# Issuing the first load of w_in ahead of the opening all-engine barrier in a single-token decode kernel

## The chip, the cores and the metric

The kernel runs on one core of a Trainium2 chip. The metric is device time in microseconds (us); lower is better.

## The reference, cut to what matters

One token of width 1024 goes through grouped-query attention over a cache (32 query heads, 4 KV heads, 65,536 positions) and through a gated MLP. A scalar gate mixes the two results.

```python
q = (x @ wq)                                   # wq: 1024 x 4096
scores = einsum(q, k) * Dh ** -0.5             # k_cache: 4 x 65536 x 128, 67 MB
a = (softmax(scores) @ v) @ wo                 # v_cache: 67 MB; wo: 4096 x 1024
z = gelu(x @ w_in)                             # w_in: 1024 x 3584
b = (z[:Fh] * (w_sp * layernorm(z[Fh:]) + b_sp)) @ w_out
out = g * a + (1 - g) * b                      # g = sigmoid(sum(x * gate_w))
```

All is bf16. Nearly every byte of the 162 MB is used once, so this is a kernel that reads memory.

## The kernel before

SyncE issues all big loads into four rotating 4 MB buffers; ScalarE issues four tiny ones. Program order on SyncE is: both halves of w_in, both halves of wq, four K tiles, w_out, then K and V tiles in turn and the last V tiles, and at the end the pieces of wo.

```python
kv = ctx.enter_context(tc.tile_pool(name="kv", bufs=NKV))          # NKV = 4

def load(src, shape, name):
    t = kv.tile([P, CT * P], BF16, name=name, tag="kv")
    ...
    nc.sync.dma_start(out=v, in_=src)
    return v
...
nc.scalar.dma_start(out=xg8[:, 0, :], in_=A_x.rearrange(...))       # 2 KB
nc.scalar.dma_start(out=xg8[:, 1, :], in_=gate_w.rearrange(...))    # 2 KB
nc.scalar.dma_start(out=wb[:, 0:1], in_=B_w_sp)                     # 2 bytes
nc.scalar.dma_start(out=wb[:, 1:2], in_=B_b_sp.unsqueeze(0))        # 2 bytes
win_t = [load(win_view[:, i * KH:(i + 1) * KH, :], (KH, F), "win_t") for i in range(2)]
wq_t = [load(wq_view[:, i * KH:(i + 1) * KH, :], (KH, HD), "wq_t") for i in range(2)]
... # xb_ps: x is spread over the partitions by a matmul; small_ps: w_sp, b_sp and the gate
z_ps = pss.tile([P, 2 * HN], FP32, name="z_ps", tag="s")
for i in range(2):
    x_rows(z_ps, win_t[i], ZN, i)              # 32 matmuls for each half of w_in
... # gelu, layernorm, q_ps from wq_t
build_w(0)
for g in range(G):
    for j in range(NT):
        k_tile(g, j, load_kv(A_k_cache, g, j, "kn"))   # the first one takes win_t[0]'s buffer
        ...
```

The framework puts an opening ahead of this code: GpSimd fills four constants, every engine drains, and an all-engine barrier follows. Only then does each engine reach its first line of the kernel.

## Time and profile before

| | before |
|---|---|
| median time of 3 runs | 385.78 us (385.75 to 385.80) |
| span of the profile | 383.9 us |
| bytes, mean rate | 162.01 MB, 422 GB/s |
| busy: load queue / TensorE / VectorE | 98.5% / 63% / 57% |

The first lines are from the page of the kernel before. The DMA row gives the busy tenths of the 16 DMA engines in 40 slices, and the GB/s row what they moved. Then come SyncE's queue (packets, MB, share of 16 engines' span) and the chain that ended last, by engine and by line.

```profile
span 383.9 us, 2650 instructions
...
DMA  8999999999999999999999999999999999999995
GB/s 335 430 437 437 435 434 430 423 431 426 428 427 437 435 430 437 427 434 430 423 432 427 437 437 422 430 434 437 427 425 427 437 438 427 425 430 431 434 411 203
...
q1 hardware_dynamic: 6192, 162.01, 98.5%
...
DMA 60%; DVE 20%; PE 11%; issue 5%; ACT 2%; SPq 1%; DVEq 0%; ACTq 0%
DMA kn<-in_A_k_cache_dram 47%; DVE kt L320 16%; DMA wo_t<-in_A_wo_dram 8%; PE s_ps L326 8%; DMA win_t<-in_B_w_in_dram 5%; DVE pt L362 2%; PE o_ps L372 2%; ACT sc L337 1%; PE z_ps L213 1%; ACT sc L359 1%; DVE mx L341 1%; DVE o_sb L387 0%; SPq L449 0%; ACT L359 0%; PE nb_ps L352 0%
```

The load queue never pauses after the first slice: the packet records hold no moment without one of its packets. (A slice can read up to 438 GB/s, because a packet counts whole in the slice in which it starts.) The trace's packet records say the same in another way: in the opening loads, once the stream has settled, a 28,672-byte packet occupies one DMA engine for 1.062 us, and 16 of these make 432 GB/s. The Trainium skill ("Perfetto Trace Analysis", Engine Utilization, Roofline) calls about 435 GB/s the ceiling of one core's 16 DMA engines; the trace agrees.

The next lines are from the view of the opening's instructions (engine, operation, count, duration in ns, first and last start in us). The letter q after an engine's name means its sequencer.

```profile
L478 POOLq EVENT_SEMAPHORE  x2: 17/17/17, 0.5 to 0.6; - x2
L478 SPq DRAIN  x1: 7/7/7, 0.0 to 0.0; - x1
...
L478 POOLq DRAIN  x1: 186/186/186, 0.3 to 0.3; - x1
...
L478 SPq EVENT_SEMAPHORE  x1: 17/17/17, 0.7 to 0.7; - x1
```

SyncE is ready at 0.0 us and passes the barrier at 0.7 us. GpSimd fills constants first, drains for 0.19 us from 0.3 us, and does its barrier steps at 0.5 to 0.6 us.

The timeline of the first 32 us of the kernel before (start, busy us, engine, line, operation, and in brackets the idle time before it and what ended it) shows what follows the barrier:

```profile
0.74 0.86 SPq L107 DMA_DIRECT2D win_t<-in_B_w_in_dram  x2
0.74 0.61 ACTq L117 DMA_DIRECT2D xg<-in_A_x_dram  x1
0.82 0.25 POOL L131 IOTA row<- 128x128 f32 x1 [0.38 <-POOLq L478]
...
7.64 0.37 PE L169 MATMUL xb_ps<-xg,spread 8*128 8x256 bf16 x1 [7.64 <-DMA xg<-in_gate_w_dram]
...
11.58 0.16 DVE L185 CAST wbf<-wb 1x2 f32<-1x2 bf16 x1 [2.12 <-DMA wb<-in_B_b_sp_dram]
...
12.30 3.18 PE L213 MATMUL z_ps<-win_t,xT 128*32 128x448 bf16 x32
...
15.54 8.36 SPq L107 DMA_DIRECT2D kn<-in_A_k_cache_dram  x2
20.34 3.18 PE L213 MATMUL z_ps<-win_t,xT 128*32 128x448 bf16 x32 [4.86 <-DMA win_t<-in_B_w_in_dram]
```

And the end of the timeline of the kernel before, where the last piece of wo decides:

```profile
380.69 0.29 PE L414 MATMUL out_ps<-wo_t,oa 128*32 128x256 bf16 x4 [0.36 <-DMA wo_t<-in_A_wo_dram]
381.02 0.37 ACT L453 CAST out_sb<-out_ps 128x256 bf16<-128x256 f32 x1 [47.61 <-PE out_ps L414]
381.43 0.61 ACTq L454 DMA_DIRECT2D out_dram<-out_sb  x1
```

### The profile page before, as it was taken

What the parts mean: (1) busy time and instruction counts of PE and PEld (TensorE: products, weight loads), DVE (VectorE), ACT (ScalarE), POOL (GpSimd) and SP (SyncE); (2) the same over time, 40 slices, a digit from 0 to 9 for tenths busy, and PEclk for the clock granted to TensorE, in tenths of its full rate; (3) what the DMA queues carried; (4) which work ended last, traced back from release to release, by engine and by line L of the source; (5) the groups of instructions that cost most, each with busy time, mean ns of one, the idle gap of its engine ahead of it and who ended that gap; (6) DMA issues with size and microseconds to landing.
All of it is one profiled execution on the core that took longest, in us unless ns stands there. A gap on an engine that the chain in (4) does not pass through costs nothing.

```text
span 383.9 us, 2650 instructions
## 1 busy us (share of the span) xinstructions
PE 242.3 (63%) x1372; PEld 59.3 (15%) x796; DVE 218.5 (57%) x211; ACT 39.6 (10%) x55; POOL 4.4 (1%) x10
## 2 busy tenths in 40 slices
PE   0433447976449948466699393774993937685553
PEld 0110001111202201011121020121220201121122
DVE  5141478988497563658975545679754546730040
ACT  1010001100511101014011010140110101400000
POOL 4000000000000000000000000000000000000000
PEclk9996559889659989686599797865997869888868
DMA  8999999999999999999999999999999999999995
GB/s 335 430 437 437 435 434 430 423 431 426 428 427 437 435 430 437 427 434 430 423 432 427 437 437 422 430 434 437 427 425 427 437 438 427 425 430 431 434 411 203
DMA packets 6248, 162.18 MB, mean 422 GB/s; under 512 B 728, under 2 KB 732, under 8 KB 1116
## 3 DMA queue, kind: packets, MB, share of 16 engines
q1 hardware_dynamic: 6192, 162.01, 98.5%
q8 instruction: 8, 0.13, 0.1%
q14 instruction: 4, 0.03, 0.0%
q10 hardware_dynamic: 44, 0.01, 0.0%
HBM read 162.01 MB, written 0.00 MB: 422 GB/s over the span
## 4 chain that ended last, share of the span: by engine, by line
DMA 60%; DVE 20%; PE 11%; issue 5%; ACT 2%; SPq 1%; DVEq 0%; ACTq 0%
DMA kn<-in_A_k_cache_dram 47%; DVE kt L320 16%; DMA wo_t<-in_A_wo_dram 8%; PE s_ps L326 8%; DMA win_t<-in_B_w_in_dram 5%; DVE pt L362 2%; PE o_ps L372 2%; ACT sc L337 1%; PE z_ps L213 1%; ACT sc L359 1%; DVE mx L341 1%; DVE o_sb L387 0%; SPq L449 0%; ACT L359 0%; PE nb_ps L352 0%
## 5 line engine op out<-in xcount | busy, mean ns | idle before, releaser
L326 PE MATMUL s_ps<-kt,wt 128*128 128x512 bf16 x512 | 142.3, 437 | 67.9 <-DVE kt L320 67.3
L320 DVE STREAM_TRANSPOSE kt<-kn 128x2048 int32<-128x2048 int32 x64 | 143.3, 2284 | 63.5 <-DMA kn<-in_A_k_cache_dram 63.4
L372 PE MATMUL o_ps<-vt,pt 128*64 128x512 bf16 x512 | 69.2, 432 | 8.8 <-DMA vt<-in_A_v_cache_dram 8.8
L326 PEld LDWEIGHTS <-wt 128*128 128x128 bf16 x256 | 27.6, 108 | 184.0 <-issue 122.9
L337 ACT CAST sc<-s_ps 128x1024 bf16<-128x1024 f32 x16 | 16.2, 1013 | 253.8 <-PE s_ps L326 253.8
L372 PEld LDWEIGHTS <-pt 128*64 128x64 bf16 x256 | 17.2, 124 | 57.9 <-issue 56.4
L362 DVE STREAM_TRANSPOSE pt<-sc 128x1024 bf16<-128x1024 bf16 x16 | 18.6, 1218 | 6.8 <-ACT sc L359 6.8
L383 DVE TENSOR_TENSOR om<-o_ps,own 128x1024 f32<-128x1024 f32 x4 | 4.8, 1205 | 26.8 <-PE o_ps L372 26.8
L359 ACT ACTIVATE sc<-sc,nb 128x1024 bf16<-128x1024 bf16 x16 | 18.2, 1139 | 10.2 <-DVE nb L355 10.2
L322 DVE TENSOR_REDUCE mx<-sc 128x1 f32<-128x1024 bf16 x12 | 14.3, 1192 | 4.4 <-ACT sc L337 4.4
L341 DVE TENSOR_REDUCE mx<-sc 128x1 f32<-128x1024 bf16 x4 | 4.9, 1220 | 12.3 <-ACT sc L337 12.3
L213 PE MATMUL q_ps<-wq_t,xT 128*32 128x512 bf16 x64 | 7.2, 630 | 7.3 <-DMA wq_t<-in_A_wq_dram 7.3
L393 PE MATMUL om_ps<-o_sb,hsel 128*32 128x128 f32 x8 | 2.4, 398 | 13.6 <-DVE o_sb L387 13.6
L213 PE MATMUL z_ps<-win_t,xT 128*32 128x448 bf16 x64 | 6.4, 577 | 4.9 <-DMA win_t<-in_B_w_in_dram 4.9
L414 PE MATMUL out_ps<-wo_t,oa 128*32 128x256 bf16 x128 | 6.3, 346 | 4.6 <-DMA wo_t<-in_A_wo_dram 3.2
L279 DVE TENSOR_TENSOR rowt<-q_ps,own_b 128x512 f32<-128x512 f32 x2 | 1.3, 686 | 12.4 <-PE q_ps L213 12.4
L345 PE MATMUL mt_ps<-ident_f,m 128*1 128x128 f32 x4 | 1.4, 346 | 10.2 <-DVE m L343 10.2
L387 DVE TENSOR_REDUCE o_sb<-om 128x128 f32<-128x1024 f32 x4 | 7.5, 1871 | 0.1
L227 DVE TENSOR_TENSOR rowt<-z_ps,own_b 128x448 f32<-128x448 f32 x2 | 1.2, 620 | 9.6 <-PE z_ps L213 9.6
L213 PEld LDWEIGHTS <-xT 128*32 128x32 bf16 x64 | 3.0, 140 | 20.3 <-issue 20.3
L453 ACT CAST out_sb<-out_ps 128x256 bf16<-128x256 f32 x1 | 0.4, 372 | 47.6 <-PE out_ps L414 47.6
L414 PEld LDWEIGHTS <-oa 128*32 128x32 bf16 x128 | 4.2, 119 | 6.9 <-issue 4.2
(88 smaller groups left out, 57.9 us busy)
## 6 DMA issues: line engine op xcount, KB each, us to landing
kn<-in_A_k_cache_dram SPq DMA_DIRECT2D x16, 4096.0 KB, 26.5
vt<-in_A_v_cache_dram SPq DMA_DIRECT2D x16, 4096.0 KB, 32.9
wq_t<-in_A_wq_dram SPq DMA_DIRECT2D x2, 4096.0 KB, 28.4
win_t<-in_B_w_in_dram SPq DMA_DIRECT2D x2, 3584.0 KB, 15.1
wo_t<-in_A_wo_dram SPq DMA_DIRECT2D x1, 4096.0 KB, 27.2
wout_t<-in_B_w_out_dram SPq DMA_DIRECT2D x1, 3584.0 KB
wo_t<-in_A_wo_dram SPq DMA_DIRECT2D x1, 2048.0 KB
wo_t<-in_A_wo_dram SPq DMA_DIRECT2D x1, 1024.0 KB
```

Source lines behind the costliest of these rows:

```text
L213: ins = nc.tensor.matmul(ps[t * B:(t + 1) * B, k * HN:k * HN + n], lhsT=xT[:, i * KH + c:i * KH + c + 1].to_broadcast([P, B]), rhs=w[:, c, ...
L320: nc.vector.transpose(out=kt[:].bitcast(I32), in_=kb[:, v * n:(v + 1) * n])
L322: nc.vector.reduce_max(**late.pop())
L326: ins = nc.tensor.matmul(s_ps[:, k * HN:(k + 1) * HN], lhsT=wt[g % 2][:, v, b].rearrange("p a v h -> p (a v h)"), rhs=kx[:, b // 2, b % 2, ...
L337: nc.scalar.copy(out=sct[g, j][:], in_=s_ps[:])
L341: nc.vector.reduce_max(**late.pop())
L359: nc.scalar.activation(out=sct[g, j][:], in_=sct[g, j][:], func=ACT.Exp, scale=SCALE, bias=nb[:, 0:1], accum_out=lss[g][:, j:j + 1])
L362: nc.vector.transpose(out=ptt[g, j][:].rearrange("p c x -> p (c x)"), in_=sct[g, j][:])
L372: ins = nc.tensor.matmul(o_ps[g][hs, e, :], lhsT=ptt[g, j][:, 2 * u:2 * u + 2, :].rearrange("p c x -> p (c x)"), rhs=vx[:, 2 * u + e], sta ...
L383: nc.vector.tensor_tensor(out=om8[:], in0=o_ps[g][:].rearrange("p e (v d) -> p (e v) d", d=DH), in1=own_8[:].unsqueeze(2).to_broadcast([P, ...
L387: nc.vector.tensor_reduce(out=o_sb[:], in_=om8[:].rearrange("p x d -> p d x"), axis=AX.X, op=ALU.add)
L414: nc.tensor.matmul(out_ps[t * B:(t + 1) * B, :], lhsT=vec[:, c0 + c:c0 + c + 1].to_broadcast([P, B]), rhs=w[:, c, t * NO:(t + 1) * NO], st ...
```

## The change

The intent is to start the stream of loads while the other engines are still on their way to the barrier. The first load writes a fresh buffer and waits for nothing, so its instruction is taken out of the kernel's block and put in front of SyncE's drain in the opening block. That nothing in the opening has to come before this load is shown only by correct results.

```diff
+    first_load = []
+
+    def start_first_load(n):
+        blocks = n.main_func.blocks
+        found = None
+        for block in blocks:
+            for i, ins in enumerate(block.instructions):
+                if ins.name in first_load:
+                    found = (block, i, ins)
+        block, i, ins = found
+        assert not ins.has_wait()
+        del block.instructions[i]
+        head = blocks[0].instructions
+        at = next(i for i, x in enumerate(head)
+                  if x.engine == ins.engine and type(x).__name__ == "InstDrain")
+        head.insert(at, ins)
+
+    nc.at_finalize(start_first_load)
+
     def load(src, shape, name):
...
-        nc.sync.dma_start(out=v, in_=src)
+        ins = nc.sync.dma_start(out=v, in_=src)
+        if not first_load:
+            first_load.append(ins.ins.name)
         return v
```

## The prediction

> **What bounds the kernel now.** The loads. The page's table of DMA queues shows SyncE's load queue occupying the 16 DMA engines for 98.5% of the span, and 162.01 MB move at a mean 422 GB/s. TensorE is busy 63%, VectorE 57%. The chain of waits gives DMA 60% of the span. SyncE waits often (159.1 us for transposes that free K buffers, by its list of waits), but it waits with about three loads queued: a load takes 26 to 33 us from issue to landing, while 4 MB take about 9.8 us at 430 GB/s. The stream is not starved: all stretches of 10 and 20 us between 40 and 370 us show 419 to 444 GB/s.
>
> **What the change does.** Nothing is added or removed. The issue of the first half of w_in (0.38 to 0.43 us of SyncE), moves from behind the opening barrier to the head of SyncE's program. The instruction list shows SyncE's drain at 0.0 us, its barrier wait of 0.7 us, and the issue at 0.74 us. The load waits for nothing, so it can start 0.7 us earlier, at about 0.0 to 0.05 us.
>
> **What lies on the critical path.** All of it: the stream is continuous, so every later transfer, and the compute behind it, should move forward equally. Checks:
> - The second half of w_in will be issued just after the barrier, at about 0.75 us, while the first half needs some 9 us of transfer: no gap.
> - Does SyncE delay the barrier? It now arrives after about 0.45 us. GpSimd, filling constants first, collects the others at 0.5 to 0.6 us: the barrier moves by at most about 0.1 us.
> - What is pushed back: the four tiny loads on ScalarE's queue. The Trainium skill ("DMA: Bandwidth & Descriptors", Queues, rings and completion order) says each DMA engine takes turns between queues at packet granularity. This trace fits: a 28 KB packet takes 1.06 us, gate_w's 2 KB wait until 7.6 us, and b_sp's value until 11.6 us. Now w_in is ahead even of x, so these landings may come 1 to 2 us later, and TensorE's first z matmuls start near 13 instead of 12.3 us. That is harmless: TensorE then sits idle for 4.9 us until the second half lands at 20.3 us, and the first K load, released by the first half's matmuls (15.5 us), has two wq loads queued ahead of it.
> - The tail is bound by the last w_o piece landing (380.64 us), then 0.3 us of matmul, a 0.37 us copy and the output store: it just shifts.
>
> **Prediction.** 385.78 - 0.7 = 385.1 us; range 384.6 to 385.7. Faster by over 2%: 0.01; within 2%: 0.98; slower by over 2%: 0.01.
>
> **What would show the steps right.** First issue near 0.0 us; the second half of w_in lands near 19.6 instead of 20.3 us; the last w_o piece near 379.9 us; the queue's share still about 98.5%. Wrong, if the first packets start late all the same, or if the 0.7 us is seen at 20 us but gone at 380 us.
>
> **What would make it wrong.** A drain on SyncE that waits for its transfer (the barrier would end near 10 us, and the time would rise about 1 to 2 us); an issue before the barrier that is itself slow; the later tiny loads exceeding their 4 us of slack; or a timing that starts with the first instruction and hides part of the shift.

## The result, and the profile after

| | before | after |
|---|---|---|
| median time (4 runs each, same rounds) | 385.79 us | 385.12 us (384.99 to 385.23) |
| ratio, 95% interval | | 0.9982 (0.9968 to 0.9996) |
| span of the profile | 383.9 us | 383.4 us |
| start of the first w_in packet, from the first instruction | 1.74 us | 1.00 us |
| first w_in packet's start to last wo packet's end | 378.43 us | 378.47 us |

A ratio is the mean time of one kernel's runs over that of the other's of the same rounds, so it is not quite the ratio of the medians. The gain is 0.67 us, and the interval excludes 1. The last two rows are worked out from the trace's DMA packet records, counted from the first instruction's record. They carry the whole story: the stream begins 0.74 us earlier and is as long as it was, within 0.04 us.

The page of the kernel after, the same lines:

```profile
span 383.4 us, 2650 instructions
...
DMA  9999999999999999999999999999999999999994
GB/s 374 436 427 427 422 432 431 438 435 437 426 434 424 422 431 434 438 434 431 429 431 427 427 431 433 438 427 427 434 429 424 431 435 434 432 427 428 431 417 193
...
q1 hardware_dynamic: 6192, 162.01, 98.6%
...
DMA 63%; DVE 19%; PE 10%; issue 5%; ACT 1%; SPq 0%; ACTq 0%; DVEq 0%
DMA kn<-in_A_k_cache_dram 53%; DVE kt L341 16%; DMA wo_t<-in_A_wo_dram 8%; PE s_ps L347 6%; DMA wb<-in_B_b_sp_dram 3%; PE o_ps L393 3%; DVE pt L383 1%; ACT sc L358 1%; PE z_ps L234 1%; DVE o_sb L408 0%; SPq L470 0%; ACT sc L380 0%; DVE mx L362 0%; DVE om L404 0%; DVE mx L343 0%
```

The first slice rises from 335 to 374 GB/s, and the rest is as before. In the chain, w_in's 5% is gone and the 2-byte load of b_sp has 3%. It looks as if a tiny load had become a limit; the experiments test that.

The opening's instructions of the kernel after (the same code has line 499 now):

```profile
L499 POOLq EVENT_SEMAPHORE  x2: 17/17/17, 0.6 to 0.7; - x2
...
L499 SPq DRAIN  x1: 126/126/126, 0.4 to 0.4; - x1
L499 SPq EVENT_SEMAPHORE  x1: 17/17/17, 0.7 to 0.7; - x1
```

SyncE now issues first and drains at 0.4 us. The drain takes 126 ns instead of 7 ns, so it does not wait for the transfer.

The timeline of the first 32 us of the kernel after:

```profile
0.00 1.11 SPq L126 DMA_DIRECT2D win_t<-in_B_w_in_dram  x2
...
0.79 0.60 ACTq L138 DMA_DIRECT2D xg<-in_A_x_dram  x1
0.87 0.25 POOL L152 IOTA row<- 128x128 f32 x1 [0.43 <-POOLq L499]
...
9.13 0.36 PE L190 MATMUL xb_ps<-xg,spread 8*128 8x256 bf16 x1 [9.13 <-DMA xg<-in_gate_w_dram]
...
11.98 0.16 DVE L206 CAST wbf<-wb 1x2 f32<-1x2 bf16 x1 [1.04 <-DMA wb<-in_B_b_sp_dram]
...
12.71 3.01 PE L234 MATMUL z_ps<-win_t,xT 128*32 128x448 bf16 x32
...
15.78 7.47 SPq L126 DMA_DIRECT2D kn<-in_A_k_cache_dram  x2
19.68 3.18 PE L234 MATMUL z_ps<-win_t,xT 128*32 128x448 bf16 x32 [3.97 <-DMA win_t<-in_B_w_in_dram]
```

ScalarE's first issue moves from 0.74 to 0.79 us: the barrier is 0.05 us later. The matmul that waits for gate_w is 1.5 us later, the first z matmuls are 0.4 us later, and the second z matmuls, which wait for data of the big stream, are 0.66 us earlier.

The end of the timeline of the kernel after:

```profile
380.02 0.40 PE L435 MATMUL out_ps<-wo_t,oa 128*32 128x256 bf16 x4 [0.25 <-DMA wo_t<-in_A_wo_dram]
380.47 0.37 ACT L474 CAST out_sb<-out_ps 128x256 bf16<-128x256 f32 x1 [47.63 <-PE out_ps L435]
380.88 0.61 ACTq L475 DMA_DIRECT2D out_dram<-out_sb  x1
```

The last four matmuls start 0.67 us earlier. The output store is issued 0.55 us earlier, because these matmuls took 0.40 instead of 0.29 us in the profiled run. The medians of the timed runs differ by 0.67 us.

### The profile page after: what moved, and what is told of

Its sections match the earlier page's. It is cut to its first block, busy times and chain, and to the rows that moved or that the text cites. A ratio compares the mean times of both kernels' runs of the same rounds, so it can differ in the third digit from the quotient of the medians.

```text
span 383.4 us, 2650 instructions
## 1 busy us (share of the span) xinstructions
PE 237.4 (62%) x1372; PEld 58.5 (15%) x796; DVE 218.3 (57%) x211; ACT 39.6 (10%) x55; POOL 4.4 (1%) x10
## 3 DMA queue, kind: packets, MB, share of 16 engines
q1 hardware_dynamic: 6192, 162.01, 98.6%
## 4 chain that ended last, share of the span: by engine, by line
DMA 63%; DVE 19%; PE 10%; issue 5%; ACT 1%; SPq 0%; ACTq 0%; DVEq 0%
DMA kn<-in_A_k_cache_dram 53%; DVE kt L341 16%; DMA wo_t<-in_A_wo_dram 8%; PE s_ps L347 6%; DMA wb<-in_B_b_sp_dram 3%; PE o_ps L393 3%; DVE pt L383 1%; ACT sc L358 1%; PE z_ps L234 1%; DVE o_sb L408 0%; SPq L470 0%; ACT sc L380 0%; DVE mx L362 0%; DVE om L404 0%; DVE mx L343 0%
## 5 line engine op out<-in xcount | busy, mean ns | idle before, releaser
L347 PE MATMUL s_ps<-kt,wt 128*128 128x512 bf16 x512 | 138.1, 425 | 73.5 <-DVE kt L341 73.4
```

The source lines that it names most:

```text
L347: ins = nc.tensor.matmul(s_ps[:, k * HN:(k + 1) * HN], lhsT=wt[g % 2][:, v, b].rearrange("p a v h -> p (a v h)"), rhs=kx[:, b // 2, b % 2, ...
```

## The experiments

The theory is that time follows the start of the big load stream one for one, and that nothing else in the opening counts. The rivals are: the gain is noise; it comes from some early DMA, whichever; the time of the barrier itself matters; later slack absorbs part of a shift; the tiny loads have become a limit, as the chain after suggests. All experiments gave correct results. The hoisting code is that of the change, for a list of instructions instead of one.

### The change again

No edit; five rounds, on the chip of the next three experiments.

> The changed kernel once more, with more rounds, on the chip of the runs below. Theory (the load stream starts 0.74 us earlier and nothing later absorbs it): 0.6 to 0.75 us less than the kernel before, about 385.1 us. Rival (the first measurement's interval nearly touched 1.0, so the gain may be noise): no clear difference.

Measured: 385.14 us (385.08 to 385.18), before 385.84 us (385.67 to 385.91), ratio 0.9982 (0.9968 to 0.9995). It is the same gain on a second set of runs, with no overlap of the two ranges. The noise rival is out.

### Only the tiny load of x is moved

```diff
-    nc.scalar.dma_start(out=xg8[:, 0, :], in_=A_x.rearrange(...))
+    ins = nc.scalar.dma_start(out=xg8[:, 0, :], in_=A_x.rearrange(...))
+    early.append(ins.ins.name)          # hoisted ahead of ScalarE's drain
```

> Only the first tiny load, x on ScalarE's queue, is moved ahead of the barrier; w_in stays behind it. Theory (only the start of the big stream counts): first 28 KB packet no earlier than before, time 385.8 us, or up to 0.15 us more if ScalarE's late arrival delays the barrier. Rival (any early DMA wakes the engines and brings the gain, or the tiny loads are what matters): about 385.1 us.

Measured: 386.38 us (386.10 to 386.47), ratio 1.0013 (1.0001 to 1.0026): 0.54 us more than before. From the timeline and the opening's instructions of this kernel:

```profile
0.14 0.60 ACTq L133 DMA_DIRECT2D xg<-in_A_x_dram  x1
...
1.16 0.88 SPq L123 DMA_DIRECT2D win_t<-in_B_w_in_dram  x2
```

```profile
L495 ACTq DRAIN  x1: 133/133/133, 0.8 to 0.8; - x1
L495 SPq EVENT_SEMAPHORE  x1: 17/17/17, 1.1 to 1.1; - x1
```

ScalarE's issue of x takes 0.60 us, so ScalarE comes last to the barrier, and SyncE's w_in issue, still behind it, moves from 0.74 to 1.16 us. The first w_in packet starts at 2.18 us, 0.44 us later than before. The direction is the theory's; my expectation had the barrier's delay too small (0.15 us), since I had not added ScalarE's start at 0.14, its issue of 0.60 and its drain of 0.13 us. In this profiled run the stream itself was also 0.13 us longer (378.56 us), which was not explained. An early DMA of the wrong kind is a loss.

### All four opening loads of SyncE are moved

The edit is shown against the change.

```diff
-        if not first_load:
-            first_load.append(ins.ins.name)
+        if len(sp_early) < 4:           # w_in twice, wq twice
+            sp_early.append(0)
+            early.append(ins.ins.name)
```

> All four opening loads on SyncE (both halves of w_in, both of wq) are moved ahead of the barrier, so SyncE arrives at it after about 1.8 us. Theory (only the first issue counts, the barrier itself does not): 385.1 us like the change, though the barrier ends near 2 us and the tiny loads come over 1 us later. Rival (a later barrier costs its delay): about 386.2 us, or at least 0.5 us more than the change.

Measured: 385.12 us (384.98 to 385.15), ratio 0.9981 (0.9968 to 0.9993). From the opening's instructions and the timeline of this kernel:

```profile
L497 SPq EVENT_SEMAPHORE  x1: 17/17/17, 2.2 to 2.2; - x1
```

```profile
2.30 0.60 ACTq L136 DMA_DIRECT2D xg<-in_A_x_dram  x1
...
17.15 0.33 SPq L123 DMA_DIRECT2D kn<-in_A_k_cache_dram  x1
```

The barrier ends at 2.2 us in this kernel's opening, ScalarE's first issue is at 2.30 us, and the first K load is issued at 17.15 us instead of 15.78 us. None of this costs anything. So a barrier 1.5 us later than the change's is free as long as the stream is already ahead of it. Together with the previous run this separates the two: the barrier matters only through what it holds back.

### The opposite dose: the first load issued late

```diff
+    rowt = big.tile([P, 2 * HN], FP32, name="rowt")      # moved up from below
+    nc.vector.memset(rowt[:], 0.0)
+    for _ in range(3):
+        nc.scalar.copy(out=rowt[:], in_=rowt[:])
...
         t = kv.tile([P, CT * P], BF16, name=name, tag="kv")
+        if not seen:
+            seen.append(0)
+            nc.scalar.copy(out=t[:, 0:1], in_=rowt[:, 0:1])   # the load must wait for this write
```

> The opposite dose on the kernel before: the first w_in load waits for three 1 us copies on ScalarE, so it is issued near 7 us instead of 0.74 us. Theory (the start of the stream counts one for one): time = 385.8 + (issue - 0.74), about 392.1 us for an issue at 7.0 us. Rival (much of a shift at the start is absorbed by slack later): less than 389 us.

Measured: 392.11 us (392.05 to 392.14), ratio 1.0162. From the timeline of this kernel:

```profile
7.04 0.84 SPq L112 DMA_DIRECT2D win_t<-in_B_w_in_dram  x2
```

The first issue was at 7.04 us and the first packet at 8.03 us. That is 6.29 us later than before, and the time is 6.27 us more. Nothing later absorbs a shift at the start, even one more than eight times as large as the change's.

### The change with all tiny loads moved too

```diff
     # on top of the change: each of the four tiny loads on ScalarE
+    early.append(ins.ins.name)
```

> The change, and the four tiny loads on ScalarE moved ahead of the barrier too. After the change the chain of waits runs through the landing of b_sp's value at 11.9 us and the first z matmuls to the first K load at 15.8 us. Theory (that part of the chain has slack, because two wq loads are still queued): 385.1 us, no gain over the change even if the first z matmuls start earlier. Rival (the chain shows a real limit): the time falls by about as much as the z matmuls start earlier, 0.5 us or more below the change.

Measured: 385.18 us (385.00 to 385.26), ratio 0.9983 (0.9970 to 0.9995). From the timeline of this kernel:

```profile
11.73 3.18 PE L236 MATMUL z_ps<-win_t,xT 128*32 128x448 bf16 x32
...
14.97 0.33 SPq L123 DMA_DIRECT2D kn<-in_A_k_cache_dram  x1
```

The first z matmuls start at 11.73 instead of 12.71 us and the first K load is issued at 14.97 instead of 15.78 us, but the time does not fall. What the chain of waits shows between 2 and 16 us is not a limit.

### The change with the tiny loads issued late

```diff
+    rowt = big.tile([P, 2 * HN], FP32, name="rowt")
+    nc.vector.memset(rowt[:], 0.0)
+    for _ in range(8):                  # 28 in the second kernel
+        nc.scalar.copy(out=rowt[:], in_=rowt[:])
     xg8 = const.tile([KC, 2, P], BF16, name="xg8")
     nc.scalar.dma_start(...)            # the four tiny loads follow
```

> The change, with the four tiny loads issued behind eight 1 us copies on ScalarE, near 11 us instead of 0.8 us; b_sp's value should land near 20 us and the first K load be issued near 24 us instead of 15.8. Theory (the K load only has to be queued before the wq loads run out near 38 us): 385.1 us. Rival 1 (the slack is the 4 us of TensorE's idle time before the second z half, as the prediction said): about 5 us more, 390 us. Rival 2 (the chain of waits shows a real limit): about 8 us more, 393 us.

Measured: 385.13 us (384.98 to 385.23), ratio 0.9982 (0.9968 to 0.9995). The timeline of this kernel:

```profile
21.63 5.89 PE L238 MATMUL z_ps<-win_t,xT 128*32 128x448 bf16 x64
24.86 3.04 SPq L126 DMA_DIRECT2D kn<-in_A_k_cache_dram  x2
```

The z matmuls start 8.9 us and the first K load 9.1 us later than in the change, and the time is the same within 0.02 us. So the "4 us of slack" of the prediction was far too small.

> The same with 28 copies: the tiny loads are issued near 31 us, land near 40 us, and the first K load is issued near 44 us. Theory (the stream runs dry near 38 us and waits): a hole of about 6 us in the DMA after 38 us and about 6 to 7 us more time, 391 to 392 us. Rival (slack of 4 us): about 25 us more, 410 us.

Measured: 394.09 us (393.74 to 395.22), ratio 1.0219 (1.0206 to 1.0233), 8.95 us more than the change by the medians. Here the slack does end. The view by windows of this kernel (window, its length, then busy us and count of PE, PEld, DVE, ACT and POOL, the granted clock, the DMA share and GB/s; a packet counts whole in the window in which it starts, so a share can exceed 1):

```profile
37.00:38.00 1.00, 0.00 (x0) 0.00 (x0) 0.00 (x0) 0.00 (x0) 0.00 (x0) 1.00 0.84 361
38.00:39.00 1.00, 0.00 (x0) 0.00 (x0) 0.00 (x0) 0.00 (x0) 0.00 (x0) 1.00 0.02 1
39.00:45.00 6.00, 4.19 (x37) 1.86 (x25) 2.66 (x16) 0.17 (x1) 0.00 (x0) 1.00 0.00 0
45.00:46.00 1.00, 1.00 (x16) 0.16 (x4) 0.00 (x0) 0.00 (x0) 0.00 (x0) 1.00 0.00 0
46.00:47.00 1.00, 1.00 (x16) 0.16 (x4) 0.00 (x0) 0.00 (x0) 0.00 (x0) 1.00 1.68 459
```

The last wq packet ends at 38.63 us, and the first K packet starts at 46.39 us: a hole of 7.8 us, and a K start 8.33 us later than the change's 38.06 us. I had expected 6 to 7 us. The K load was issued at 45.42 instead of near 44 us, and I had left out the 0.98 us from issue to first packet. For the remaining 0.6 us (8.95 - 8.33), the packet records of the profiled run point to the restart of the stream: counted from the first K packet, in order of their starts, packet 16 is 8.86 us, packet 128 8.92 us and packet 256 8.93 us later than the same packet of the change. This profiled run, the slowest of the four (395.22 us), loses about 1 us more among its last 128 packets (9.01 to 10.08 us later); why it does was not traced.

### The runs together

| kernel | first w_in packet, us | shift against before | median time, us | difference to before of the same rounds |
|---|---|---|---|---|
| before | 1.74 | 0 | 385.84 | 0 |
| after (again) | 1.00 | -0.74 | 385.14 | -0.70 |
| four opening loads early | 1.00 | -0.74 | 385.12 | -0.72 |
| change, tiny loads early too | 0.99 | -0.75 | 385.18 | -0.66 |
| change, tiny loads 8 copies late | 1.01 | -0.74 | 385.13 | -0.71 |
| only x early | 2.18 | +0.44 | 386.38 | +0.54 |
| first load late | 8.03 | +6.29 | 392.11 | +6.27 |

The packet starts are from one profiled run each. Over seven kernels the time follows the start of the stream to within about 0.1 us. The kernel with 28 copies is the one that leaves this line, and it does so because the stream itself has a hole. No version was found that beats the change by more than the scatter: SyncE's first instruction is already the load.

## Why the prediction was right

The predicted time was 385.1 us; 385.12 and 385.14 us were measured.

- **The bound.** The load stream was named as the bound; the shift carried to the end (0.74 us at the first packet, 0.70 at the last, 0.67 in the time), and the late load shows the same for a shift of 6.29 us. Right, and shown.
- **The 0.7 us.** The issue moved from 0.74 to 0.00 us and the first packet from 1.74 to 1.00 us. Right, and shown. The other checks that it named came out too: the z matmuls that wait for the second half of w_in start at 19.68 us, the last piece of wo has landed at 379.98 us, and the queue's share is 98.6%. The Trainium skill ("DMA: Bandwidth & Descriptors", Latency and other measured facts) gives a first-byte time of about 0.6 us for this kind of queue; here the first packet starts 1.00 us after the issue starts, and 0.63 us after it ends (the issue took 0.38 us).
- **The barrier.** At most 0.1 us later was predicted; 0.05 us was measured. The feared drain took 126 ns. That its time does not matter was only implied; the run with four loads shows it.
- **The tiny loads.** 1 to 2 us later was predicted. It was 1.5 us for gate_w, but only 0.4 us for b_sp, so the first z matmuls started at 12.71 and not near 13 us. The packet records show where b_sp caught up. The value of w_sp, the 4-byte packet behind it, b_sp's value and its 4-byte packet start at 7.85, 9.01, 10.08 and 11.14 us before, one to each big packet's time of 1.06 us, but at 9.42, 10.49, 10.50 and 11.56 us after: two of them go together, which saves one such turn. Why they did was not tested.
- **The slack.** This step was mis-sized. The prediction took TensorE's idle time of 4.9 us before the second z half as the limit ("4 us of slack"). The eight-copy run used up 9 us at no cost; the limit is the moment when the queued wq loads run out, 38.6 us. The prediction had named these queued loads in the same sentence and should have used them.
- **The tail.** "It just shifts" held for the landing of wo (0.66 us); in the profiled pair 0.11 us was lost in the last matmuls. The profiled run of the change (385.20 us) is the second slowest of its four; the medians give 0.67 us.

## What to carry to other kernels

Where a continuous stream of loads is the bound, its first issue is on the critical path, and a load that waits for nothing does not have to stand behind an opening barrier: moving it gave nearly all of the 0.74 us that it had waited, 0.67 and 0.70 us in two sets of runs. Choose the engine and the load with care, because an early issue on an engine that then comes late to the barrier delays everything that is still behind it (0.54 us lost with the tiny load of x). And don't take the chain of waits as a list of limits: ask how much is queued at the DMA engines, for here a load issued behind two others was late by 9 us and cost nothing.

## What the Trainium skill lacked or had wrong

- No page tells that a DMA without waits may be issued before a program's opening barrier, or what that is worth: 0.67 to 0.70 us here. The place would be "DMA: Bandwidth & Descriptors", Rules for kernel authors.
- "Perfetto Trace Analysis" names a drain as an instruction of the sequencer but does not say whether a drain behind a DMA issue waits for the transfer. Here it did not: 126 ns on SyncE and 133 ns on ScalarE behind one issue, 125 ns and 239 ns behind four, against 7 to 8 ns without one.
- "DMA: Bandwidth & Descriptors", Queues, rings and completion order, states the turns between queues but no cost. Here two loads of 2 KB and two of 2 bytes ran beside a stream of 28 KB packets (1.06 us each), and the copy that waits for the last of them started 10.8 us after the first was issued (0.74 to 11.58 us) in the kernel before, and 11.3 us after (9.62 to 20.90 us) in the run with eight copies. Without the stream beside them, in the run with the first load late, the last packet of the same four loads ended at 2.88 us instead of 11.15 us.
- The first-byte figure of about 0.6 us on the same page fits the SyncE loads looked at only if it is counted from the end of the issue (0.62 to 0.66 us); counted from its start it was 0.98 to 1.02 us. For x on ScalarE, whose issue takes 0.60 us, neither count fits: 0.98 us from the start and 0.37 us from the end in the kernel before.
